# Head 0's q and k joined on SBUF, its turned tile read four times, and eleven heads with values in split halves instead of four

## The chip, the cores and the metric

One core of a Trainium2 chip runs the whole program. The metric is device time in microseconds of one execution; three executions of the kernel before gave a median of 781.59 us (781.08 to 782.19). The core's engines are TensorE (PE in the tables, its weight loads PEld), VectorE (DVE), ScalarE (ACT), GpSimd (POOL) and SyncE (SP, which here only issues DMAs).

## The reference

The program is an attention with a hash mask, followed by two feed-forward blocks on the 1536 tokens that it gives.

```python
q_bits = (einsum('bhsd,dk->bhsk', q, proj) > 0)        # 6 bits each, of q and of k
mask   = q_bucket[:, :, :, None] == k_bucket[:, :, None, :]
scores = where(mask, q @ k.T / sqrt(64), -1e9)         # 2 batches x 8 heads, 768 x 768
attn   = softmax(scores); y = attn @ v                 # head dim 64
x = y as 1536 x 512
h = x @ w_in; g = h * tanh(softplus(h)); x = g @ w_out         # 512 -> 2048 -> 512
out = ((x @ w1) * (x @ w2)) @ w3 @ w_out2                      # 512 -> 1024 -> 1024 -> 512
```

## The kernel before

Heads are counted from 0 to 15. For each head `load_head` brings q and k side by side into one SBUF tile `rw` (128 rows of 6 x 2 x 64), and `prep` makes the features: TensorE turns the tile (L514) so that q stands on the lower 64 partitions and k on the upper 64; a high and a low part are cut from the turned tile (`hh` and `ll`, both in tiles named `hh`, L532 and L534); six DMAs move halves of these into `qb`, `kb`, `qa`, `ka` (L480); three matmuls per half with `psel2` give the hash bits (L565), which VectorE compares (L576) into further rows of `qa`, and one more DMA copies these rows to `ka`. Head 0 has a form of its own (L547 to L555): ScalarE and VectorE write its features straight from the turned tile, in twelve reads, and its bits take four matmuls per half with a matrix `psel`.

`scores` computes one of six row blocks of a head (L606: two matmuls `kb,qb` and two `ka,qa` of 384 columns), VectorE takes the row maximum (L619) and ScalarE the exponential with its row sum (L622). `unit` turns three blocks of `E` (L666) and copies the 128 x 384 result `T` out of PSUM; either ScalarE or VectorE copies (L443). `values` multiplies by v (L695) in one of two forms. A head in the list `FRV` (the bits of `fm`) has split halves: T is copied as a rounded high part, VectorE subtracts the low part (L675), v is cut into high and low columns of one tile (L475), and a pair of T blocks takes four matmuls with 128 stationary columns. Any other head has two matmuls in plain fp32 with 64 stationary columns each, one into the lower and one into the upper 64 rows of the result; the trace shows two records for each of these.

Beside the heads runs work that doesn't depend on them: weights come in as 1 MB chunks and are decoded to fp32 (`decode`, L733 to L747), stored, fetched again and cut into high and low parts (`split`, L796 and L798); `wprod` multiplies w3 and w_out2 (L846); `ff_first` does the feed-forward of the first 512 tokens (L1049, L1065, L1160) while later heads are still at work. The remaining 1024 tokens follow (L1005, L1419, L1461).

The order on every engine is fixed at build time by a planner (`Plan`): each unit of work has a cost, a due time and the buffers that it needs, and the planner places units one by one. Each engine then runs its list strictly in order. The numbers in `CFG` set due times, buffer limits and penalties, so a change of one of them can reorder the lists of all engines.

```python
FRV = [x for x in range(NH) if CFG["fm"] >> x & 1]       # 120: heads 3 to 6
P.op("PE", 0.70 if u in FRV else 0.93, mm, ...)          # values, a pair of T blocks
```

Of the kernel before, what the change touches and what calls it, by code (L numbers as in the profile page):

```python
# [8 lines left out]
F32 = mybir.dt.float32  # L9
# [29 lines left out]
    "hl": 3,  # L39
# [13 lines left out]
    "eg": 0,  # L53
    "xqd": 120.04,
# [5 lines left out]
    "fm": 120,  # L60
# [260 lines left out]
def kernel(  # L321
# [88 lines left out]
    psel = ctile([128, 2, 2, 128], "psel", FR)  # L410
# [11 lines left out]
    v_id, v_psel, v_psel2, v_ccol, v_qks = Val(), Val(), Val(), Val(), Val()  # L422
# [62 lines left out]
    def prep(u, d0, step):  # L485
# [39 lines left out]
        if u:
            for x in ((slice(0, 2), ) if t.one else (slice(0, 1), slice(1, 2))):
                n = (x.stop - x.start) * HS
                cols = slice(x.start * HS, x.stop * HS)
                key = t.all()[x]
                src = (lambda t=t: t.v[0]()[:, :, 0:HS]) if t.one else (lambda t=t, x=x: t.at(x.start))  # L530
                dst = (lambda v_: half(v_())) if t.one else (lambda v_, cols=cols: v_()[:, cols])
                P.op("ACT", act(n) + 0.01, lambda src=src, dst=dst: nc.scalar.activation(  # L532
                    out=dst(hh), in_=src(), func=AF.Copy, scale=qks[:, 0:1]), r=key + [v_qks], w=[(hh, x.start)], due=d(1.3), name=f"hh{u}")
                P.op("DVE", dve(n), lambda src=src, dst=dst: nc.vector.scalar_tensor_tensor(  # L534
                    out=dst(ll), in0=src(), scalar=qks[:, 0:1], in1=dst(hh), op0=ALU.mult, op1=ALU.subtract),
                    r=key + [(hh, x.start), v_qks], w=[(ll, x.start)], due=d(1.6), name=f"ll{u}")
            for o, to, f, fr in ((qb, low, hh, low), (kb, high, hh, high), (qa, low, hh, low), (ka, low, hh, high),
                                 (qb, high, ll, low), (kb, low, ll, high)):
                move(o, to, f, fr, [f], [(o, to.start if o in (qb, kb) else "x")], d(2.2), f"fa{u}")
            ops = [(psel2[:, 0], hh), (psel2[:, 1], hh), (psel2[:, 0], ll)]  # L540
            needs = [hh, ll, v_psel2]
        else:
            inv = 1.0 / float(D) ** 0.5
            for a in range(2):
                cols = slice(a * HS, (a + 1) * HS)
                for o, p, fr, c in ((kb, high, high, inv), (ka, low, high, inv), (qb, low, low, 1.0)):
                    P.op("ACT", act(HS), lambda t=t, o=o, p=p, fr=fr, c=c, a=a, cols=cols: nc.scalar.activation(  # L547
                        out=o()[p, cols], in_=t.at(a)[fr], func=AF.Copy, scale=c), r=[t.key(a)],
                        w=[(o, ("x" if o is ka else p.start, a))], due=d(1.3 + 0.3 * a), name=f"hh{u}")
                P.op("DVE", dve(HS), lambda t=t, a=a, cols=cols: nc.vector.tensor_copy(out=qa()[low, cols], in_=t.at(a)[low]),  # L550
                     r=[t.key(a)], w=[(qa, ("x", a))], due=d(1.3 + 0.3 * a), name=f"hh{u}")
                P.op("DVE", dve(HS), lambda t=t, a=a, cols=cols: nc.vector.tensor_sub(
                    out=qb()[high, cols], in0=t.at(a)[low], in1=qa()[low, cols]), r=[t.key(a), (qa, ("x", a))],
                    w=[(qb, (D, a))], due=d(1.4 + 0.3 * a), name=f"ll{u}")
                P.op("DVE", dve(HS), lambda t=t, a=a, cols=cols: nc.vector.scalar_tensor_tensor(  # L555
                    out=kb()[low, cols], in0=t.at(a)[high], scalar=inv, in1=kb()[high, cols],
                    op0=ALU.mult, op1=ALU.subtract), r=[t.key(a), (kb, (D, a))], w=[(kb, (0, a))], due=d(1.5 + 0.3 * a), name=f"ll{u}")
            ops = [(psel[:, 0, 0], qb), (psel[:, 1, 0], kb), (psel[:, 0, 1], qb), (psel[:, 1, 1], kb)]
            needs = [qb, kb, v_psel]
# [7 lines left out]
        for a in range(2):  # L567
            r = needs if u else [(qb, (x, a)) for x in (0, D)] + [(kb, (x, a)) for x in (0, D)] + [v_psel]
# [18 lines left out]
        for a in range(2):  # L587
# [3 lines left out]
                 r=[(qa, ("m", a))], w=[(ka, ("m", a))], due=d(4.6), name=f"km{u}")  # L591

# [34 lines left out]
    def norm(u, due):  # L627
# [25 lines left out]
        P.op("SP", 0.5, lambda: nc.sync.dma_start(  # L653
# [161 lines left out]
    def wprod(f, d0, d1):  # L815
# [40 lines left out]
        P.op("SP", 0.5, lambda: nc.sync.dma_start(out=wp_d[f * 128:(f + 1) * 128], in_=o()[:, 0:DM]), r=[o], w=[(v_wp, f)],  # L856
# [9 lines left out]
    def x_split(n, due, after=()):  # L866
# [3 lines left out]
        for kk in range(KD):  # L870
# [5 lines left out]
            for e in range(2):  # L876
                P.op("SP", 0.5, lambda e=e, kk=kk, rb=rb: nc.sync.dma_start(
# [62 lines left out]
    def x_quarters(due, after=()):  # L940
        xs = []
        for i in range(2):
            xq_ = Quarters()
            xs.append(xq_)
            for n in (1, 2):
                t0, t1 = n * TB, (n + 1) * TB
                bs = range(t0 // S, (t1 - 1) // S + 1)
                for k1 in range(2):
# [5 lines left out]
                    for e in range(2):  # L954
                        P.op("SP", 0.5, lambda e=e, kk=kk, rb=rb, t0=t0, t1=t1: nc.sync.dma_start(
# [114 lines left out]
    def ff_first(n, d0, d1):  # L1070
# [107 lines left out]
        def o_group(G):  # L1178
# [3 lines left out]
            for t4 in range(TB // 128):  # L1182
# [360 lines left out]
```

## Time and profile before

| | us |
|---|---|
| median of three executions | 781.59 |
| the profiled execution, own time | 781.81 |
| its span | 780.0 |
| PE busy | 765.0 |
| DVE busy | 557.8 |
| ACT busy | 508.9 |

The page gives for each engine the time in which it had an instruction running. TensorE's instructions overlap, so its busy time says only when it was not empty: how fast it went is read from the distance between starts. VectorE's and ScalarE's records overlap by a little as well. The first matmul of head 0's scores starts at 14.8 us, that of head 1 at 28.3, of head 3 at 67.0, of head 7 at 174.4, of head 9 at 213.1, of head 12 at 299.2 and of head 15 at 386.9; the table of stretches in the rows below is cut at these times.

### The profile page before, as it was taken

Reading aid. Unit: us, or ns where it says so; the run is one execution under the profiler, and the core shown is the slowest. Engines: PE = TensorE matmul, PEld = TensorE weight load, DVE = VectorE, ACT = ScalarE, POOL = GpSimd, SP = SyncE. Lnnn points to the kernel's source line nnn. Section 1 sums busy time; section 2 is a strip of 40 time slices with the busy share of each in tenths; the row PEclk is TensorE's granted clock in tenths of the full one; section 3 lists DMA queues with packets and bytes.
Section 4 is the critical chain, followed back from the end, with each engine's and each line's share of the span. In section 5 each row is a group of like instructions: output and inputs, shape, how many; then the busy total and the mean of one; then the engine's idle time right before and its main releaser. Section 6 shows DMA issues by size and latency. Waiting matters only on the chain.

```text
span 780.0 us, 10577 instructions
## 1 busy us (share of the span) xinstructions
PE 765.0 (98%) x3808; PEld 596.7 (76%) x3808; DVE 557.8 (72%) x812; ACT 508.9 (65%) x815; POOL 105.4 (14%) x204
## 2 busy tenths in 40 slices
PE   6999999999999999999999999999999999999998
PEld 5767888897577777777766888888888888788877
DVE  3897778889877986967996959764543848775620
ACT  3889667779799887868867835654544626443330
POOL 3222001222332222113212110000000000000000
PEclk8999999999999999999999999999999999999999
DMA  6997646697897768755465740431215310010011
GB/s 206 214 305 229 181 128 200 157 336 218 259 280 220 249 207 255 230 175 165 158 230 203 259 147 28 162 103 39 75 54 162 109 54 1 28 54 1 1 54 55
DMA packets 62252, 120.70 MB, mean 155 GB/s; under 512 B 29924, under 2 KB 32324, under 8 KB 61176
## 3 DMA queue, kind: packets, MB, share of 16 engines
q1 hardware_dynamic: 45944, 55.02, 25.4%
q0 software_dynamic: 16256, 65.02, 24.2%
q8 instruction: 30, 0.49, 0.3%
q14 instruction: 22, 0.18, 0.1%
HBM read 83.89 MB, written 17.87 MB: 130 GB/s over the span
## 4 chain that ended last, share of the span: by engine, by line
PE 91%; DVE 4%; ACT 2%; issue 1%; DMA 1%; SPq 0%; ACTq 0%; DVEq 0%
PE q L1005 20%; PE b L1419 11%; PE b L1065 9%; PE s L606 8%; PE b L695 8%; PE b L666 7%; PE b L1160 6%; PE b L1049 5%; PE b L846 5%; PE b L1461 5%; PE s L565 2%; PE s L514 1%; PE b L829 1%; DVE st L619 1%; DMA ka<-qa 1%
## 5 line engine op out<-in xcount | busy, mean ns | idle before, releaser
L1005 PE MATMUL q<-k,k 128*128 128x512 f32 x672 | 159.4, 395 | 0.0
L1005 PEld LDWEIGHTS q<-k,k 128*128 128x128 f32 x672 | 126.1, 188 | 30.4 <-DVE f L1020 0.4
L798 DVE TENSOR_TENSOR k<-f,k 128x1024 fp32r<-128x1024 f32 x92 | 111.7, 1220 | 20.5 <-ACT k L796 20.2
L796 ACT CAST k<-f 128x1024 fp32r<-128x1024 f32 x92 | 94.7, 1050 | 21.0 <-DVE f L988 6.4
L619 DVE TENSOR_REDUCE st<-s 128x1 f32<-128x768 f32 x96 | 90.9, 950 | 21.7 <-PE s L606 19.4
L622 ACT ACTIVATE E<-s,st 128x768 f32<-128x768 f32 x96 | 86.9, 905 | 25.1 <-DVE st L619 15.2
L666 PE MATMUL b<-ident,E 128*128 128x128 f32 x576 | 92.0, 274 | 0.2 <-DVE T L675 0.2
L1016 ACT COPY f<-q 128x512 f32<-128x512 f32 x64 | 37.5, 586 | 81.6 <-PE q L1005 78.6
L1020 DVE TENSOR_TENSOR f<-q,f 128x512 f32<-128x512 f32 x64 | 42.9, 686 | 65.8 <-PE q L1005 39.5
L1419 PE MATMUL b<-k,k 128*128 128x512 f32 x384 | 89.6, 393 | 0.0
L666 PEld LDWEIGHTS b<-ident,E 128*128 128x128 f32 x576 | 71.4, 140 | 23.7 <-issue 7.2
L1419 PEld LDWEIGHTS b<-k,k 128*128 128x128 f32 x384 | 72.1, 188 | 16.6
L1065 PE MATMUL b<-k,k 128*128 128x512 f32 x288 | 78.2, 404 | 0.0
L1065 PEld LDWEIGHTS b<-k,k 128*128 128x128 f32 x288 | 51.5, 188 | 15.2 <-issue 6.0
L695 PE MATMUL b<-T,v 128*64 128x384 f32 x288 | 62.4, 511 | 0.0
L606 PE MATMUL s<-kb,qb 128*128 128x384 f32 x192 | 56.7, 376 | 1.4 <-ACT E L622 1.1
L1049 PE MATMUL b<-k,k 128*128 128x512 f32 x192 | 54.5, 407 | 0.0
L443 ACT COPY T<-b 128x384 f32<-128x384 f32 x94 | 43.9, 483 | 15.2 <-PE b L666 13.8
L846 PE MATMUL b<-k,k 128*128 128x512 f32 x192 | 52.1, 405 | 0.0
L606 PE MATMUL s<-ka,qa 76*128 76x384 f32 x192 | 49.9, 341 | 0.6 <-DMA ka<-qa 0.6
L1160 PE MATMUL b<-k,k 128*128 128x512 f32 x192 | 47.4, 396 | 0.0
L1461 PE MATMUL b<-k,f 128*128 128x512 f32 (+1 forms) x216 | 46.4, 370 | 0.8 <-ACT f L1451 0.5
(143 smaller groups left out, 1117.7 us busy)
## 6 DMA issues: line engine op xcount, KB each, us to landing
k<-in_moe_w_dram POOLq DMA_DIRECT2D x16, 1024.0 KB, 5.9
k<-in_moe_w_out_dram POOLq DMA_DIRECT2D x12, 1024.0 KB, 7.8
k<-in_moe_w_in_dram POOLq DMA_DIRECT2D x8, 1024.0 KB, 8.0
f<-keep_wo SPq DMA_DIRECT2D x16, 512.0 KB
qb<-hh SPq DMA_DIRECT2D x30, 192.0 KB
kb<-hh SPq DMA_DIRECT2D x30, 192.0 KB
keep_wi<-f POOLq DMA_DIRECT2D x8, 512.0 KB, 7.0
f<-keep_wi POOLq DMA_DIRECT2D x8, 512.0 KB, 7.0
```

The source lines that it names most:

```text
L606: nc.tensor.matmul(t()[:, a, 0:HS], lhsT=l()[0:kk, i * 128:(i + 1) * 128], rhs=r()[0:kk, a * HS:(a + 1) * HS], start=(l is qb), stop=(l is ...
L619: P.op("DVE", 0.868, lambda: nc.vector.tensor_reduce(out=s()[:, 0, i:i + 1], in_=t()[:, :, 0:HS], axis=AX.XY, op=ALU.max, negate=True), r= ...
L666: nc.tensor.transpose(t()[:, ci * 128:(ci + 1) * 128], es[ci]()[:, kt * 128:(kt + 1) * 128], ident)
L695: nc.tensor.matmul(t()[r, 0:HS], lhsT=w, rhs=f(), start=first and j == 0, stop=last and j == CH - 1)
L796: P.op("ACT", act(1024, True), lambda: nc.scalar.copy(out=hl()[:, 0:1024], in_=f()), r=[f], w=[(hl, 0)], due=due, name="hi")
L798: vec(0, 1024, lambda v_: v_.tensor_sub(out=hl()[:, 1024:2048], in0=f(), in1=hl()[:, 0:1024]), r=[f, (hl, 0)], w=[(hl, 1)], due=due + 0.1, ...
L846: nc.tensor.matmul(acc(), lhsT=hv()[:, ws, g_, :], rhs=wview(wo2[g_ // 2], 2)[:, rs, g_ % 2, :], start=(n == 0), stop=(n == 3 * GT - 1))
L1005: nc.tensor.matmul(qs[q](), lhsT=lhs(w, i), rhs=xs[i].at(xs[i].hl[x], o), start=first and n == 0, stop=n == 5, skip_group_check=True)
L1049: nc.tensor.matmul(of(), lhsT=wview(w, KD)[:, ws, kk, (f % 2) * 128:(f % 2) * 128 + 128], rhs=kview(xhl[n][kk // 2], xs, kk), start=(m == ...
L1065: nc.tensor.matmul(of(), lhsT=l(), rhs=rr(), start=(m == 0), stop=(m == len(ops) - 1))
L1160: nc.tensor.matmul(t(), lhsT=wview(w, KD)[:, ws, kk, f2 * 128:f2 * 128 + 128], rhs=kview(x2[kk // 2], xs, kk), start=(kk == 0 and s == 0), ...
L1419: nc.tensor.matmul(t(), lhsT=wview(w, 2)[:, ws, f, dd * 128:(dd + 1) * 128], rhs=gv[:, gs, f, :], start=(j == 0 and f == 0 and s == 0), st ...
```

## The change

Head 0's q and k are loaded as whole rows into one tile `f`, and two VectorE copies join them into `rw`. Head 0 then goes the way of all other heads: its turned tile is read four times (two halves of `hh` by ScalarE, two of `ll` by VectorE), its bits take three matmuls per half with `psel2`; `psel` is gone, and `psel2` is filled by GpSimd from `proj`. The four halves of `qb` and `kb` are copied by ScalarE and VectorE, those of `qa` and `ka` are moved by DMA. Heads 2 to 6 and 8 to 13 have values in split halves (`fm` 16252), eleven heads. Other numbers of `CFG` change too, so that the planner's order is another on every engine; `low` 29 gives w3's chunks the decoding with two VectorE operations and w_out2's the one with one, where `low` 30 had it the other way.

```diff
-    "prep": 11.28,
-    "wp0": 16.52,
-    "wp1": 41.2,
-    "dec0": 47.78,
-    "dec1": 116.06,
+    "prep": 10.55,
+    "wp0": 16.46,
+    "wp1": 45.62,
+    "dec0": 40.08,
+    "dec1": 121.7,
...
-    "hl": 3,
+    "hl": 4,
...
-    "pen": 0.4,
-    "low": 30,
+    "pen": 0.19,
+    "low": 29,
...
-    "fm": 120,
+    "fm": 16252,
...
+            if u == 0:
+                row = lambda x=x: f()[:, x * C * D:(x + 1) * C * D].rearrange("p (c d) -> p c d", c=C)
+                P.op("SP", 0.65, lambda row=row, src=src: nc.sync.dma_start(
+                    out=row(), in_=src[b, h].rearrange("(p c) d -> p c d", c=C)), w=[(f, nm)], due=due, lat=1.5, name=f"load{nm}{u}")
+                P.op("DVE", dve2(C * D), lambda x=x, row=row: nc.vector.tensor_copy(out=t()[:, :, x], in_=row()), r=[(f, nm)],
+                     w=[(t, nm)], due=due, name=f"join{u}")
+                continue
...
-            for a in range(2):
-                cols = slice(a * HS, (a + 1) * HS)
-                for o, p, fr, c in ((kb, high, high, inv), (ka, low, high, inv), (qb, low, low, 1.0)):
-                    P.op("ACT", act(HS), lambda t=t, o=o, p=p, fr=fr, c=c, a=a, cols=cols: nc.scalar.activation(
-                        out=o()[p, cols], in_=t.at(a)[fr], func=AF.Copy, scale=c), r=[t.key(a)],
-                        w=[(o, ("x" if o is ka else p.start, a))], due=d(1.3 + 0.3 * a), name=f"hh{u}")
...
-            ops = [(psel[:, 0, 0], qb), (psel[:, 1, 0], kb), (psel[:, 0, 1], qb), (psel[:, 1, 1], kb)]
...
+        for o, to, f, fr, e in ((qb, low, hh, low, "ACT"), (kb, high, hh, high, "ACT"), (qa, low, hh, low, ""), (ka, low, hh, high, ""),
+                                (qb, high, ll, low, "DVE"), (kb, low, ll, high, "DVE")):
+            w = [(o, to.start if o in (qb, kb) else "x")]
+            if u or not e:
+                move(o, to, f, fr, [f], w, d(2.2), f"fa{u}", None if u else 2.0)
+            else:
+                P.op(e, act(S, True) if e == "ACT" else dve2(S), lambda o=o, to=to, f=f, fr=fr, e=e: copy(e, o()[to], f()[fr]), r=[f], w=w,
+                     due=d(2.2), name=f"fa{u}")
+        ops = [(psel2[:, 0], hh), (psel2[:, 1], hh), (psel2[:, 0], ll)]
```

What stands on VectorE at the start of the program, before the first row maximum, in the kernel before (`s_74` is the turned tile of head 0, `s_75` its bits):

```order
L1244 COPY ccol<-b_67 128x2
L550 CAST qa_89<-s_74 64x384
L1249 CAST pq<-prow 128x6
L1250 TENSOR_TENSOR pq<-prow,pq 128x6
L1251 TENSOR_SCALAR pq<-pq 128x12
L1255 COPY psel<-pq 128x2x6 x4
L552 TENSOR_TENSOR qb_85<-s_74,qa_89 64x384
L555 SCALAR_TENSOR_TENSOR kb_87<-s_74,kb_87 64x384
L550 CAST qa_89<-s_74 64x384
L555 SCALAR_TENSOR_TENSOR kb_87<-s_74,kb_87 64x384
L552 TENSOR_TENSOR qb_85<-s_74,qa_89 64x384
L576 TENSOR_SCALAR qa_89<-s_75,ccol 64x384 x2
```

And in the changed kernel, in the same place:

```order
L456 COPY rw_95<-f_148 128x6x64 x2
L1238 COPY ccol<-b_67 128x2
L542 SCALAR_TENSOR_TENSOR hh_94<-s_74,qks,hh_93 128x384 x2
L442 COPY qb_85<-hh_94 64x768
L442 COPY kb_87<-hh_94 64x768
L570 TENSOR_SCALAR qa_89<-s_75,ccol 64x384 x2
L614 TENSOR_REDUCE st_106<-s_74 128x1
```

The six reads of the turned tile by VectorE have become two, with the two joins ahead of them and two copies behind them; ScalarE's six reads have become two as well.

TensorE in head 11, around one pair of the values of head 10, before:

```order
L666 MATMUL b_70<-ident,E_84 128x128
L695 MATMUL b_67<-T_2769,v_97 64x384
L695 MATMUL b_67<-T_2796,v_97 64x384
L1065 MATMUL b_68<-k_2468,k_2594 128x512 x3
L1065 MATMUL b_69<-k_2468,k_2594 128x512 x3
```

And in the changed kernel (`f_2791` holds v in two parts):

```order
L601 MATMUL s_75<-ka_92,qa_90 128x384 x2
L690 MATMUL b_70<-T_2839,f_2791 128x384
L690 MATMUL b_70<-T_2849,f_2791 128x384
L690 MATMUL b_70<-T_2855,f_2791 128x384
L690 MATMUL b_70<-T_2872,f_2791 128x384
L661 MATMUL b_69<-ident,E_79 128x128
```

Two matmuls of 64 stationary columns have become four of 128, of the same 384 columns.

VectorE in head 11, from its first row maximum, before:

```order
L619 TENSOR_REDUCE st_108<-s_75 128x1
L443 COPY T_2753<-b_67 128x384
L1125 TENSOR_TENSOR k_2542<-b_70,k_2542 128x512
L443 COPY mvs<-b_68 64x1
L443 COPY T_2769<-b_67 128x384
L619 TENSOR_REDUCE st_108<-s_74 128x1
```

And in the changed kernel:

```order
L614 TENSOR_REDUCE st_108<-s_74 128x1
L670 TENSOR_TENSOR T_2849<-b_67,T_2839 128x384
L442 CAST T_2855<-b_69 128x384
L793 TENSOR_TENSOR k_2821<-f_2414,k_2821 128x1024
L670 TENSOR_TENSOR T_2872<-b_69,T_2855 128x384
L442 CAST T_2876<-b_67 128x384
L633 RECIPROCAL st_107<-st_107 128x6
L670 TENSOR_TENSOR T_2883<-b_67,T_2876 128x384
L1120 TENSOR_TENSOR k_2631<-b_68,k_2631 128x512
L614 TENSOR_REDUCE st_108<-s_75 128x1
```

Between two row maxima there now stand eight operations where four stood.

## Rows read from the trace of the kernel before

**Rows 1.** The page: span, and busy time of the engines.

```profile
span 780.0 us, 10577 instructions
PE 765.0 (98%) x3808; PEld 596.7 (76%) x3808; DVE 557.8 (72%) x812; ACT 508.9 (65%) x815; POOL 105.4 (14%) x204
```

**Rows 2.** Busy by stretch: PE, PEld, DVE, ACT, POOL; clock, DMA share, GB/s.

```profile
0.00:14.80 14.80, 7.38 (x23) 5.56 (x24) 4.25 (x14) 4.50 (x8) 6.76 (x28) 0.90 0.56 146
14.80:28.30 13.50, 13.50 (x75) 12.04 (x75) 9.97 (x14) 8.93 (x20) 0.00 (x0) 0.86 0.87 248
28.30:67.00 38.70, 37.97 (x225) 25.23 (x223) 35.30 (x49) 35.84 (x68) 11.16 (x21) 1.00 0.91 263
67.00:174.40 107.40, 107.40 (x631) 92.42 (x629) 86.23 (x135) 77.94 (x143) 19.05 (x37) 1.00 0.68 205
174.40:213.10 38.70, 36.94 (x221) 27.02 (x219) 36.88 (x57) 32.12 (x65) 10.34 (x20) 1.00 0.78 242
213.10:299.20 86.10, 85.42 (x450) 61.58 (x449) 65.69 (x90) 76.65 (x117) 22.51 (x38) 1.00 0.80 235
299.20:386.90 87.70, 87.70 (x465) 63.27 (x463) 68.74 (x98) 71.05 (x111) 20.49 (x38) 1.00 0.64 201
386.90:780.00 393.10, 388.67 (x1734) 309.58 (x1732) 250.72 (x359) 201.87 (x289) 15.07 (x24) 1.00 0.27 91
```

**Rows 3.** Timeline of the start: start us, us, engine, line, what.

```profile
5.15 1.51 PE L514 MATMUL s<-ident,rw 128*128 128x128 f32 x6 [1.56 <-DMA rw<-in_k_dram]
6.70 0.48 ACT L547 ACTIVATE kb<-s 64x384 fp32r<-64x384 f32 x1 [4.38 <-PE s L514]
...
12.70 0.55 DVE L552 TENSOR_TENSOR qb<-s,qa 64x384 fp32r<-64x384 f32 x1
...
15.06 1.29 DVE L576 TENSOR_SCALAR qa<-s,ccol 64x384 fp32r<-64x384 f32 x2 [1.80 <-PE s L565]
...
16.40 0.58 ACT L532 ACTIVATE hh<-b,qks 128x384 fp32r<-128x384 f32 x1
...
17.01 0.62 DVE L534 SCALAR_TENSOR_TENSOR hh<-b,qks,hh 128x384 fp32r<-128x384 f32 x1 [0.67 <-ACT hh L532]
...
18.02 0.77 PE L606 MATMUL s<-ka,qa 76*128 76x384 f32 x2
...
18.83 1.82 DVE L619 TENSOR_REDUCE st<-s 128x1 f32<-128x768 f32 x2
```

**Rows 4.** Timeline of TensorE around a plain pair of values, head 9.

```profile
236.36 0.49 PE L666 MATMUL b<-ident,E 128*128 128x128 f32 x3
236.78 0.87 PE L695 MATMUL b<-T,v 128*64 128x384 f32 x4
237.58 0.62 PE L606 MATMUL s<-kb,qb 128*128 128x384 f32 x2
```

**Rows 5.** Timeline of TensorE around a split pair, head 3.

```profile
93.61 0.51 PE L606 MATMUL s<-ka,qa 76*128 76x384 f32 x2
93.96 0.86 PE L695 MATMUL b<-T,f 128*128 128x384 f32 x4
94.66 0.49 PE L666 MATMUL b<-ident,E 128*128 128x128 f32 x3
```

**Rows 6.** The chain that ended last: start us, us, what.

```profile
1.48 3.54 DMA rw<-in_k_dram
...
53.01 0.99 PE b L666 x9
...
175.56 0.93 DVE T L675 x2
...
207.36 6.78 DMA ka<-qa
...
429.94 11.12 PE b L1160 x48
```

**Rows 7.** Groups by line: what, xcount | busy us, mean ns | idle before.

```profile
L744 DVE TENSOR_SCALAR k<-f 128x1024 int32<-128x1024 int32 x4 | 2.8, 698 | 0.7 <-ACT f L733 0.7
```

More of the change, by code (lines that the diff above doesn't have):

```diff
@@ L42 @@
     "hlk": 2,
-    "ahead": 12.45,
-    "clk": 120.94,
-    "pen": 0.4,
-    "low": 30,
-    "vdue": 2.94,
+    "ahead": 10.58,
+    "clk": 126.8,
+    "pen": 0.19,
+    "low": 29,
+    "vdue": 2.6,
     "va": 0,
@@ L52 @@
     "tb": 2,
-    "eg": 0,
-    "xqd": 120.04,
+    "eg": 1,
+    "xqd": 110,
     "p0": 2,
@@ L476, in load_v, with move @@
                  r=[t, (g, "hi")], w=[(g, "lo")], due=u * C + CFG["vdue"] + 0.1, name=f"vl{u}")
-    def move(o, to, f, fr, r, w, due, name):
-        P.op("SP", 0.5, lambda: nc.sync.dma_start(out=o()[to].bitcast(F32), in_=f()[fr].bitcast(F32)),
-             r=r, w=w, due=due, lat=5.0, name=name)
+    def move(o, to, f, fr, r, w, due, name, lat=None):
+        P.op("SP", 0.65, lambda: nc.sync.dma_start(out=o()[to].bitcast(F32), in_=f()[fr].bitcast(F32)),
+             r=r, w=w, due=due, lat=lat or 5.0, name=name)
     first_bits = []
@@ L514, in tr @@
                 nc.tensor.transpose(t.at(a)[:, i * 128:(i + 1) * 128], raw()[:, c].rearrange("p s d -> p (s d)"), ident)
-        hh, ll = (Val(HH, "h"), Val(HH, "l")) if u else (None, None)
-        if u and t.one:
+        hh, ll = Val(HH, "h"), Val(HH, "l")
+        halves = not (u and t.one)
+        if not halves:
             P.op("PE", C * 0.118, tr, r=[raw], w=t.all() + [(hh, "t"), (ll, "t")], due=d(1), name=f"tq{u}", after=first_bits)
@@ L521, in prep @@
                 P.op("PE", CH * 0.118, lambda t=t, a=a: tr(t, range(a * CH, (a + 1) * CH)), r=[raw],
-                     w=[t.key(a)] + ([(hh, "t"), (ll, "t")] if u and not a else []), due=d(1), name=f"tq{u}", after=first_bits if u else ())
+                     w=[t.key(a)] + ([] if a else [(hh, "t"), (ll, "t")]), due=d(1), name=f"tq{u}", after=first_bits if u else ())
         low, high = slice(0, D), slice(D, 2 * D)
         half = lambda v_: v_.rearrange("p (a n) -> p a n", a=2)
[L525 to L543, printed above, removed]
-            for a in range(2):
-                cols = slice(a * HS, (a + 1) * HS)
-                for o, p, fr, c in ((kb, high, high, inv), (ka, low, high, inv), (qb, low, low, 1.0)):
-                    P.op("ACT", act(HS), lambda t=t, o=o, p=p, fr=fr, c=c, a=a, cols=cols: nc.scalar.activation(
-                        out=o()[p, cols], in_=t.at(a)[fr], func=AF.Copy, scale=c), r=[t.key(a)],
-                        w=[(o, ("x" if o is ka else p.start, a))], due=d(1.3 + 0.3 * a), name=f"hh{u}")
[L550 to L557, printed above, removed]
-            ops = [(psel[:, 0, 0], qb), (psel[:, 1, 0], kb), (psel[:, 0, 1], qb), (psel[:, 1, 1], kb)]
-            needs = [qb, kb, v_psel]
@@ new lines, in prep @@
+        for x in (slice(0, 1), slice(1, 2)) if halves else (slice(0, 2), ):
+            n = (x.stop - x.start) * HS
+            cols = slice(x.start * HS, x.stop * HS)
+            key = t.all()[x]
+            src = (lambda t=t, x=x: t.at(x.start)) if halves else (lambda t=t: t.v[0]()[:, :, 0:HS])
+            dst = (lambda v_, cols=cols: v_()[:, cols]) if halves else (lambda v_: half(v_()))
+            P.op("ACT", act(n) + 0.15, lambda src=src, dst=dst: nc.scalar.activation(
+                out=dst(hh), in_=src(), func=AF.Copy, scale=qks[:, 0:1]), r=key + [v_qks], w=[(hh, x.start)],
+                due=d(1.3 + 0.1 * x.start), name=f"hh{u}")
+            P.op("DVE", dve(n), lambda src=src, dst=dst: nc.vector.scalar_tensor_tensor(
+                out=dst(ll), in0=src(), scalar=qks[:, 0:1], in1=dst(hh), op0=ALU.mult, op1=ALU.subtract),
+                r=key + [(hh, x.start), v_qks], w=[(ll, x.start)], due=d(1.4 + 0.1 * x.start), name=f"ll{u}")
@@ L567, in prep @@
         for a in range(2):
-            r = needs if u else [(qb, (x, a)) for x in (0, D)] + [(kb, (x, a)) for x in (0, D)] + [v_psel]
+            r = ([(hh, a), (ll, a)] if halves else [hh, ll]) + [v_psel2]
             P.op("PE", pe(HS, len(ops)), lambda a=a: bits(a), r=r, w=[t.key(a)], due=d(4), name=f"bits{u}")
@@ L591, in prep @@
                  r=[(qa, ("m", a))], w=[(ka, ("m", a))], due=d(4.6), name=f"km{u}")
+        first_bits.append(P.units[-1])
     E, st, et, pv = {}, {}, {}, {}
```

47 lines of the change are left out of this document (20 added, 27 removed).

## The prediction

> **What bounds the kernel now.** I read the page's busy times first, then the table of stretches, then the timeline of the start, then TensorE's timeline around the values. TensorE is never empty for long (765.0 of 780.0), VectorE is busy 557.8 [rows 1]. The stretches say more [rows 2]. From 386.9 on TensorE has 388.7 of 393.1 and VectorE 250.7: a pure TensorE tail, 48 matmuls of 512 columns in 11.12 us, 0.232 each [rows 6]. In heads 3 to 6, 9 to 11 and 12 to 14 TensorE is full, VectorE at 80%, 76% and 78%. In heads 1 to 2 and 7 to 8 VectorE is the fullest or nearly so (35.3 and 36.9 of 38.7). Before 14.8 us there is a wait for head 0's features, and TensorE's clock is granted at a mean of 0.90 there and 0.86 in the next stretch, so part of both ran at the lower of its two levels, after TensorE had sat idle between head 0's pieces.
>
> **The start.** Before: k lands at 1.48 + 3.54 = 5.02 [rows 6], the turning starts at 5.15, the reads of the turned tile run from 6.70 to 12.70 + 0.55 = 13.25, the compare starts at 15.06, the second half of the first scores at 18.02, the first maximum at 18.83 [rows 3]. Twelve reads in 6.55 us is 0.55 each, one after another, although two engines share them.
> Now four reads. ScalarE's cost 0.58 and VectorE's 0.62 on this shape [rows 3], together 2.4 us instead of 6.55: 4.1 saved. The bits lose one matmul in four. Against it, two joins stand behind the loads; their form is not in the trace, so 0 to 1.3 us (two of VectorE's 0.62), and the loads themselves may land 0 to 1 us sooner as whole rows; I take both as even. VectorE has two copies of 768 columns ahead of the compare; bounded by nothing and two reads of 0.62, I take 0.9. The new DMAs of `qa` and `ka` can start when the second ScalarE read ends, at 6.70 + 2 x 0.58 = 7.9. A move of that kind with others in flight took 6.78 us, a first load of the program 3.54 [rows 6], so they land between 11.4 and 14.7. The old gap from the compare to the maximum was 18.83 - 15.06 = 3.8 us; the new compare starts near 6.70 + 2.4 + 0.9 + 0.9 (bits) = 10.9, its maximum near 14.7 or earlier. So the first maximum comes at 12 to 15.3 where it came at 18.83: 3.5 to 6.8 gained. I take 5, near the middle, as both ends are the same wait.
> How much of that reaches head 1 depends on head 1's moves, which follow on the same queue and meet the first weight chunks; VectorE also has one v low part and one half of `ll` more in head 0. Bounds 2 and 6.5; I keep **-5.0**.
> The Trainium skill (PSUM — Partial Sum Buffer, PSUM bank collisions raise a hardware error) says that a dependency is added between two engines that touch one bank and quadrant, reads included. That agrees with the strict turns of the twelve reads. By bank alone the two halves could be read side by side, which would end the four reads some 1.2 us sooner; the trace shows turns across both halves, so the sum doesn't use it.
>
> **Values in split halves, TensorE.** A plain pair: three transposes cost 0.33 (nine in 0.99 [rows 6]), and from 236.36 to 237.58 three of them and the pair take 1.22, so the pair takes 0.89 [rows 4]. A split pair takes 94.66 - 93.96 = 0.70 [rows 5]. Seven more heads have six pairs each: 42 x 0.19 = 8.0 us less for TensorE.
> A page speaks against this part: the Trainium skill (TensorEngine Tiling (Array Packing), Theoretical Speedup) gives a stationary side of 64 up to twofold speed, as two tiles work side by side, and the split form gives that up. By that rule alone TensorE would gain nothing here; the rows have the plain pair slower by 0.19, and I go by them.
>
> **Values in split halves, VectorE.** Twelve subtractions more per head, 84. Two in a row take 0.93, 0.465 each [rows 6]: 39 us. In the order VectorE also gets nine copies of T more (4.2) and seven low parts of v, which have the shape of a T subtraction (3.3). `low` moves four operations of 0.70 to VectorE (2.8, [rows 7]) and four of ScalarE's away. That is about +49 us on VectorE with ScalarE somewhat relieved. Whether this costs anything is decided by stretch; I counted the instructions of each head in both orders, cut at the first maximum on VectorE and the first scores on TensorE.
> Heads 1 to 2: VectorE +5 subtractions, +9 copies, -3 decode operations: 6.5 - 2.1 = +4.4, so 39.7 in a stretch of 38.7 that had 3.4 idle. At least +1, at most +4.4; I take **+2**.
> Heads 3 to 6: 24 matmuls of `wprod` (5.6) and 8 transposes (0.9) move out to later heads, the values stay as they are: TensorE 107.4 to 101. VectorE 86.2 + 6 = 92 is still below. **-6.4**.
> Heads 7 to 8: that work arrives here, TensorE +6. VectorE gets 5 subtractions, a copy, two decode merges (1.1 each), a `split`, a compare, two low parts of w3, a v low part and some of the x work, about +10: 46.8 for a stretch of 38.7 that was 95% busy. It must grow, by 5 to 8; I take **+6.5**.
> Heads 9 to 11: VectorE +34 subtractions and a little, 65.7 + 16.8 = 82.5; TensorE 16 split pairs (11.3) for 17 plain ones (15.1) and small things, 86.1 - 4.1 = 82.0. Both engines need the same; with two us of waiting 84: **-2**, bounds -4 and +2.
> Heads 12 to 14: VectorE 68.7 + 18 = 87, TensorE 87.7 - 2.8 = 84.9: 88, **+0.3**, bounds -3 and +5.
> From head 15 on the order has three matmuls more and three transposes fewer: **+0.4**.
> For heads 7 to 14 that is 46.8 + 82.5 + 87 = 216 busy on VectorE against the 212.5 that the stretch took. The base rows count the end of each record in full, some 0.08 that a next one would cover (0.55 for a read that follows at 0.465), so a VectorE without idle time needs 6 or 7 us less, about 209. I end at 45.2 + 84 + 88 = 217, 4% above that.
>
> **Sum.** -5.0 + 2 - 6.4 + 6.5 - 2 + 0.3 + 0.4 = -4.2. The profiled execution took 781.81, so 777.6; the median shown, 781.59, is 0.2 below that execution, which I don't correct for.
>
> **Rivals.**
> VectorE fits in everywhere, as `split` and x work can wait: all of TensorE's 8.0 comes through beside the start's 5.0, 768.8. For it: VectorE's total after is about 607 of 780. Against it: each engine keeps its list, and a subtraction ahead of a row maximum holds up the next scores.
> The start's gain is lost before head 3: heads 1 and 2 have DMA at 0.91, ScalarE at 35.8 and VectorE at 35.3 of 38.7 [rows 2], and head 1's moves are as late as the weights make them. Then 781.8 + 0.8 = 782.6. Against it: the 4 us come off a chain in which two engines took turns, and DMA stands at 0.56 before 14.8 us [rows 2].
> Slower: VectorE bounds heads 7 to 14. It needs 216 of busy time, and where it was fullest before (heads 7 to 8) it was 95.3% busy, as it waits for transposes and for ScalarE's copy ahead of each subtraction. 216 / 0.953 = 227, 14.5 more than 212.5; with -6.4, +2, +0.4 and -5 that is 787. It decides from the point at which VectorE is busy less than 97.5% there (216 / 0.975 = 221.5, which eats 9.0). For it: eight operations between two maxima in head 11. Against it: head 3 to 6's split heads ran at 80% without stopping TensorE.
>
> **Chances.** The forecast 0.47 (773 to 781), all of TensorE's gain 0.17, the start lost 0.20, slower 0.16. About 0.2% (1.6 us) is what a measurement of this kernel can tell from none. Faster: 0.17 + 0.40 + 0.03 = 0.60; within 0.2%: 0.06 + 0.14 = 0.20; slower 0.01 + 0.03 + 0.16 = 0.20. The range 769 to 786 leaves about half of the first rival and half of the last outside.
>
> **What would show it.** The first maximum at 12 to 15.3 us and head 1's first scores near 23; the `T,f` group on TensorE 264 strong at about 0.18 from start to start; VectorE near 605 in all and above 95% in heads 7 to 14; heads 3 to 6 about 101 us, heads 7 to 8 about 45. I am wrong if head 1 starts after 26, or if TensorE waits for VectorE in heads 9 to 14 by more than a few us.

## The result and the profile after

The changed kernel takes 790.68 us (median of 4 runs, 789.06 to 791.35) where the kernel before takes 781.47 beside it: a ratio of 1.0113, 95% interval 1.0100 to 1.0125. It is slower by 9.2 us; the forecast was 4.2 faster, and the range ended at 786.

The page of the profiled execution after (790.65 us), busy time by engine and the clock in 40 slices, against [rows 1]:

```profile
span 788.9 us, 10671 instructions
PE 766.1 (97%) x3809; PEld 622.2 (79%) x3809; DVE 604.2 (77%) x911; ACT 504.5 (64%) x805; POOL 105.5 (13%) x206
...
PEclk9999999999989999989999999999999999999999
```

VectorE has gained 46.4 us of busy time, near the 49 of the forecast. TensorE has lost none, although each split pair is shorter than the plain one it replaces. The clock row has a fall to 8 in two slices in the middle; the one before had none there.

The same stretches, cut at the first scores of heads 0, 1, 3, 7, 9, 12 and 15 (stretch, its length, PE, PEld, DVE, ACT, POOL busy, clock, DMA share, GB/s), answer [rows 2]:

```profile
0.00:9.30 9.30, 6.28 (x20) 4.98 (x20) 3.11 (x8) 4.30 (x6) 5.54 (x27) 1.00 0.70 171
9.30:26.20 16.90, 14.17 (x75) 12.08 (x75) 10.63 (x15) 8.86 (x19) 1.94 (x5) 0.90 0.93 254
26.20:64.50 38.30, 37.02 (x222) 25.85 (x222) 37.58 (x56) 35.04 (x62) 9.85 (x19) 1.00 0.94 273
64.50:168.10 103.60, 102.55 (x604) 89.53 (x602) 91.69 (x147) 70.12 (x136) 17.47 (x37) 1.00 0.61 194
168.10:214.90 46.80, 43.12 (x253) 33.72 (x251) 45.10 (x72) 40.88 (x73) 13.42 (x27) 1.00 0.99 304
214.90:302.20 87.30, 84.58 (x446) 71.42 (x445) 81.17 (x127) 72.00 (x111) 20.64 (x36) 0.96 0.75 218
302.20:394.10 91.90, 88.59 (x471) 74.66 (x470) 88.56 (x144) 71.16 (x115) 23.31 (x36) 0.96 0.59 179
394.10:788.90 394.80, 389.79 (x1733) 310.01 (x1731) 246.39 (x350) 202.19 (x288) 13.29 (x22) 1.00 0.26 88
```

Read it by differences:

| stretch | before | after | change | forecast |
|---|---|---|---|---|
| to head 1's first scores | 28.3 | 26.2 | -2.1 | -5.0 |
| heads 1 to 2 | 38.7 | 38.3 | -0.4 | +2 |
| heads 3 to 6 | 107.4 | 103.6 | -3.8 | -6.4 |
| heads 7 to 8 | 38.7 | 46.8 | +8.1 | +6.5 |
| heads 9 to 11 | 86.1 | 87.3 | +1.2 | -2 |
| heads 12 to 14 | 87.7 | 91.9 | +4.2 | +0.3 |
| the rest | 393.1 | 394.8 | +1.7 | +0.4 |
| sum | | | +8.9 | -4.2 |

In heads 7 to 14 VectorE is busy 45.10 + 81.17 + 88.56 = 214.8 of 226.0 us, 95.0%.

The start after, from its timeline (start us, us, engine, line, what), answers [rows 3]:

```profile
4.10 1.54 PE L521 MATMUL s<-ident,rw 128*128 128x128 f32 x6 [0.29 <-DVE rw L456]
...
9.23 1.29 DVE L570 TENSOR_SCALAR qa<-s,ccol 64x384 fp32r<-64x384 f32 x2
...
13.21 0.59 PE L601 MATMUL s<-ka,qa 76*128 76x384 f32 x2 [1.80 <-DMA ka<-hh]
...
13.84 0.96 DVE L614 TENSOR_REDUCE st<-s 128x1 f32<-128x768 f32 x1 [3.32 <-PE s L601]
...
15.88 0.95 DVE L614 TENSOR_REDUCE st<-s 128x1 f32<-128x768 f32 x1
...
16.25 2.27 PE L559 MATMUL b<-hh,psel 128*128 128x384 f32 x6
...
19.45 0.96 DVE L614 TENSOR_REDUCE st<-s 128x1 f32<-128x768 f32 x1 [0.21 <-PE s L601]
...
24.65 0.58 ACT L539 ACTIVATE hh<-b,qks 128x384 fp32r<-128x384 f32 x1 [0.48 <-DMA ka<-hh]
...
26.17 0.62 PE L601 MATMUL s<-kb,qb 128*128 128x384 f32 x2 [0.26 <-ACT E L617]
```

A piece of the start's chain of waits, and a stretch of the start (columns as above):

```profile
17.00 7.46 DMA ka<-hh
```

```profile
15.20:18.70 3.50, 2.98 (x11) 3.01 (x12) 2.46 (x5) 2.02 (x5) 0.00 (x0) 0.51 1.09 358
```

The first maximum comes at 13.84 instead of 18.83, 5.0 sooner. Head 1's bit matmuls then stand between head 0's second and third maximum: 15.88 to 19.45 is 3.57 us. The granted clock is at its lower level there: the six bit matmuls take 2.27 us, and 1.29 in the profile of the run without subtractions below, where it isn't. Head 1's first scores wait for head 0's last exponentials, and these stand behind a feature copy of head 2 that waited for head 1's move `ka`, which was under way for 7.46 us.

TensorE in head 9, now with split values, answers [rows 4, 5]: from 238.97 to 239.68 the four matmuls of a pair take 0.71.

```profile
238.97 0.86 PE L690 MATMUL b<-T,f 128*128 128x384 f32 x4
239.68 0.86 PE L1044 MATMUL b<-k,k 128*128 128x512 f32 x3
```

Four stretches of heads 9 and 13 (columns as above), then the matmuls that waited ahead of the two falls, from TensorE's timeline, then two pieces of the chain of waits:

```profile
214.90:223.50 8.60, 7.18 (x39) 5.84 (x37) 8.54 (x12) 4.99 (x11) 5.39 (x8) 1.00 1.01 229
223.50:230.30 6.80, 6.42 (x18) 4.87 (x19) 5.47 (x9) 5.53 (x9) 1.14 (x2) 0.50 1.02 377
...
333.90:339.50 5.60, 3.90 (x23) 3.28 (x21) 5.60 (x9) 4.68 (x9) 2.97 (x6) 1.00 1.01 270
339.50:346.30 6.80, 6.29 (x17) 4.86 (x18) 5.89 (x9) 4.05 (x8) 3.64 (x5) 0.50 0.68 245
```

```profile
221.72 0.62 PE L601 MATMUL s<-kb,qb 128*128 128x384 f32 x2 [0.60 <-ACT E L617]
...
223.75 1.70 PE L661 MATMUL b<-ident,E 128*128 128x128 f32 x6 [1.06 <-DVE T L670]
...
338.33 0.61 PE L601 MATMUL s<-kb,qb 128*128 128x384 f32 x2 [1.49 <-ACT E L617]
```

```profile
226.01 3.78 PE b L1044 x8
...
231.80 1.38 PE b L1044 x6
```

In 8.6 us VectorE is busy for 8.54 and TensorE stands idle for 1.4 of them: scores wait 0.60 for an exponential that follows a late maximum, and transposes wait 1.06, part of it in the next stretch, for a subtraction that still reads the PSUM tile that they write. In the 5.6 us ahead of the second fall scores wait 1.49 for an exponential. Then the granted clock is at its lower level, 1.2 GHz, for 6.8 us from 223.5, and again from 339.5. Eight matmuls of 512 columns take 0.473 each at the lower level, six take 0.230 each after it.

### The profile page after: what moved, and what is told of

Read it like the earlier page. It is cut to its first block, busy times and chain, and to the rows that moved or that the text cites. A ratio compares the mean times of both kernels' runs of the same rounds, so it can differ in the third digit from the quotient of the medians.

```text
span 788.9 us, 10671 instructions
## 1 busy us (share of the span) xinstructions
PE 766.1 (97%) x3809; PEld 622.2 (79%) x3809; DVE 604.2 (77%) x911; ACT 504.5 (64%) x805; POOL 105.5 (13%) x206
## 4 chain that ended last, share of the span: by engine, by line
PE 70%; DVE 19%; DMA 3%; issue 3%; ACT 3%; SPq 1%; POOL 0%; ACTq 0%; DVEq 0%; POOLq 0%
PE q L1000 20%; PE b L1405 11%; PE b L1060 6%; PE b L1155 6%; PE b L1447 5%; PE b L841 5%; PE b L1044 5%; PE b L690 4%; DVE st L614 4%; PE b L661 3%; PE s L601 3%; DVE T L670 3%; DVE T L442 2%; DMA k<-in_moe_w_in_dram 2%; DVE k L793 1%
## 5 line engine op out<-in xcount | busy, mean ns | idle before, releaser
L791 ACT CAST k<-f 128x1024 fp32r<-128x1024 f32 x92 | 94.6, 1048 | 23.5 <-PE b L1060 8.9
L1015 DVE TENSOR_TENSOR f<-q,f 128x512 f32<-128x512 f32 x64 | 42.9, 687 | 67.3 <-PE q L1000 41.4
L1405 PE MATMUL b<-k,k 128*128 128x512 f32 x384 | 90.2, 395 | 0.0
L661 PEld LDWEIGHTS b<-ident,E 128*128 128x128 f32 x576 | 70.8, 141 | 24.5 <-issue 4.8
L670 DVE TENSOR_TENSOR T<-b,T 128x384 fp32r<-128x384 f32 x132 | 70.9, 547 | 6.6 <-ACT T L442 5.6
L1060 PE MATMUL b<-k,k 128*128 128x512 f32 x288 | 74.2, 399 | 0.2
L601 PE MATMUL s<-kb,qb 128*128 128x384 f32 x192 | 54.9, 367 | 7.0 <-ACT E L617 3.5
L690 PE MATMUL b<-T,f 128*128 128x384 f32 x264 | 61.4, 354 | 0.3 <-DVE T L670 0.2
L1044 PE MATMUL b<-k,k 128*128 128x512 f32 x192 | 56.6, 427 | 0.9 <-DVE k L1120 0.7
L841 PE MATMUL b<-k,k 128*128 128x512 f32 x192 | 53.7, 406 | 1.3 <-DVE k L832 1.1
L442 ACT CAST T<-b 128x384 fp32r<-128x384 f32 x76 | 35.6, 479 | 22.5 <-PE b L661 20.9
L690 PEld LDWEIGHTS b<-T,f 128*128 128x128 f32 x264 | 46.4, 192 | 3.0 <-DVE T L670 1.4
```

Source lines behind the costliest of these rows:

```text
L601: nc.tensor.matmul(t()[:, a, 0:HS], lhsT=l()[0:kk, i * 128:(i + 1) * 128], rhs=r()[0:kk, a * HS:(a + 1) * HS], start=(l is qb), stop=(l is ...
L661: nc.tensor.transpose(t()[:, ci * 128:(ci + 1) * 128], es[ci]()[:, kt * 128:(kt + 1) * 128], ident)
L670: P.op("DVE", dve(HS), lambda: nc.vector.tensor_sub(out=f[1](), in0=t()[:, 0:HS], in1=f[0]()), r=[t, f[0]], w=[f[1]], due=due, name=f"TL{u ...
L690: nc.tensor.matmul(t()[r, 0:HS], lhsT=w, rhs=f(), start=first and j == 0, stop=last and j == CH - 1)
L791: P.op("ACT", act(1024, True), lambda: nc.scalar.copy(out=hl()[:, 0:1024], in_=f()), r=[f], w=[(hl, 0)], due=due, name="hi")
L841: nc.tensor.matmul(acc(), lhsT=hv()[:, ws, g_, :], rhs=wview(wo2[g_ // 2], 2)[:, rs, g_ % 2, :], start=(n == 0), stop=(n == 3 * GT - 1))
```

## The experiments

Heads "added" are those that the change gives split values: 2 and 8 to 13. Where it says "order held", every instruction that remains stands where the changed kernel has it (or the kernel before, if that is named).

### The set of split heads alone, planned anew

```
changed kernel:     "fm": 16252,  ->  "fm": 120,
kernel before:      "fm": 120,    ->  "fm": 16252,
changed kernel:     all of the planner's numbers as before
```

> The changed kernel with fm 120, so that only heads 3 to 6 have values in split halves; all else as changed, and the planner makes its own order from it. Theory V (VectorE binds heads 7 to 14 because of the 84 added subtractions): 778 to 783, since VectorE loses some 39 us of work and TensorE gets its 8 us back. Rival P (the other due times of CFG crowd decoding and weight loads, whatever the values do): 787 to 791.

> The kernel before with fm 16252 alone: eleven heads in split halves, the old start, the old CFG otherwise. V: 787 to 794, VectorE busy 95% or more in heads 8 to 14. P: 774 to 780, as TensorE saves 8.0 and nothing else is changed.

> The changed kernel with the whole CFG of before: only head 0's load, features and bits are the new ones. Both theories: 776 to 781, the start's gain of 2 to 5 us and no more. If the start's gain doesn't reach later heads, 781 to 783.

Measured: 794.3 us (ratio 1.0159, 1.0143 to 1.0174), 801.34 (1.0247, 1.0232 to 1.0262) and 788.58 (1.0086, 1.0069 to 1.0102). All three forecasts missed. In the third, which has the start's new code and the old numbers of `CFG`, head 1 starts at 25.6 and keeps 2.7 us of gain, but the planner orders the later heads anew: head 9 takes 36.2 us (211.8 to 248.0) where it took 27.3. The costs that the planner counts with are part of the change too, in the code and not in `CFG` (0.65 for the issue of a DMA by SyncE where it was 0.5), and they stay new in the first and third run. A planner that is run again moves everything, and costs here more than the term that was to be isolated. So these runs say nothing of a single part, and the next ones hold the order.

### No subtractions in the added heads, order held

```
-   nc.vector.tensor_sub(out=f[1](), in0=t()[:, 0:HS], in1=f[0]())
+   None if u in ADDED else nc.vector.tensor_sub(...)
-   fs[x][s]
+   fs[x][0 if u in ADDED else s]
```

The values of the added heads lack the low part of T; TensorE does the same matmuls.

> The changed kernel with its planned order, but the subtractions of the seven added heads (2 and 8 to 13) are not issued, and their matmuls read the high part twice, so these heads lack the low part of the weights' product. TensorE's instructions are the same in number and shape. V: 769 to 777, VectorE falls under 85% in heads 9 to 14, and the clock's dips near 223 and 339 us go. P: 785 or more, since the order and all loads stay.

Measured: 780.69 us (778.96 to 782.03; ratio 0.9983, 0.9971 to 0.9994), 10.0 us less than the changed kernel. Heads 7 to 8, 9 to 11 and 12 to 14:

```profile
167.00:212.70 45.70, 42.70 (x252) 33.83 (x251) 43.58 (x67) 40.65 (x73) 13.63 (x26) 1.00 1.00 306
212.70:296.70 84.00, 81.19 (x446) 69.64 (x446) 67.39 (x96) 71.80 (x111) 19.78 (x38) 1.00 0.81 232
296.70:382.80 86.10, 84.31 (x471) 72.67 (x470) 73.87 (x107) 70.43 (x115) 22.07 (x37) 1.00 0.61 190
```

The clock is at its upper level throughout these stretches. The time lies between the two expectations. The subtractions cost 10.0 us, nearly all of it in heads 9 to 14 (179.2 to 170.1). Even so the kernel beats the one before by 1.3 us only, not by the 5 to 13 that were expected: what the new order does to the other stretches stays.

### Plain values in the added heads, order held

```
-   f = Val(TP, "T", dt=FR if u in FRV else F32), ...
+   f = Val(TP, "T", dt=FR if u in FRV and u not in ADDED else F32), ...
+   if u in ADDED: one plain matmul per chunk, no subtraction (of T or of v)
```

> The changed kernel with its planned order held, but the values of the seven added heads in the plain form: no subtraction, T and v in fp32, two matmuls of 64 stationary columns for a pair. It computes the reference. V (VectorE's subtractions cost more than TensorE's shorter pairs give): 781 to 787, that is below the changed kernel's 790.7, VectorE under 90% in heads 9 to 14. If the split halves gain on balance and only the new order costs: 792 to 798.

Measured: 789.7 us (786.98 to 795.89; ratio 1.0101, 1.0075 to 1.0127), between the two expectations; the interval holds the changed kernel's 1.0113. Heads 9 to 11 and 12 to 14:

```profile
215.20:301.40 86.20, 84.83 (x447) 61.10 (x445) 66.20 (x92) 71.53 (x111) 20.22 (x36) 1.00 0.77 222
301.40:391.10 89.70, 88.58 (x471) 63.25 (x469) 73.02 (x105) 70.76 (x115) 22.40 (x37) 1.00 0.59 183
```

TensorE is busy 173.4 us here in heads 9 to 14, and 165.5 in the run without subtractions: the plain form costs it 7.9 us, and the whole kernel 9.0. So the split values give TensorE what was forecast (8.0), and VectorE's subtractions take 10.0: about even. The Trainium skill (TensorEngine Tiling (Array Packing), Theoretical Speedup) gives the plain form, with its stationary side of 64, up to twofold speed; by that rule TensorE would have gained nothing from the split, and these two runs differ by 7.9. The change's 9.2 us are then not in that exchange but in what came with it, the new order above all, which has 46.4 us in heads 7 to 8 even here. The order was planned for the short pairs; what plain pairs lose by that is not shown.

### Added subtractions in the kernel before, its order held

```
+   after each second copy of T in heads 2 and 8 to 13:
+   nc.vector.tensor_sub(out=scr, in0=f[0](), in1=f[0]())
```

84 subtractions into a tile that nobody reads.

> The kernel before with its order held, and behind every copy of T of heads 2 and 8 to 13 one more VectorE subtraction of the same shape into a scratch tile (from SBUF, so no bank of PSUM is held longer): 84 operations that nothing waits for. V: 787 to 796, as VectorE needs some 207 of the 212.5 us of heads 7 to 14. If VectorE has room: 781 to 784.

Measured: 790.52 us (790.22 to 790.96; ratio 1.0105, 1.0088 to 1.0122), as theory V had it. Heads 7 to 8, 9 to 11 and 12 to 14, against [rows 2]:

```profile
176.40:215.60 39.20, 37.21 (x220) 27.06 (x219) 38.87 (x62) 31.23 (x63) 10.15 (x20) 1.00 0.80 242
215.60:304.40 88.80, 86.65 (x451) 61.34 (x450) 81.41 (x125) 77.38 (x119) 24.72 (x39) 1.00 0.80 229
304.40:396.30 91.90, 88.85 (x465) 63.11 (x463) 84.34 (x131) 71.42 (x111) 20.05 (x38) 1.00 0.59 189
```

39 us of VectorE's work cost 9 us, and VectorE is only 92% busy in heads 9 to 14. It need not be full to cost time, nor does the clock have to fall (1.00 in all three). Nothing waits for the added operations themselves; they make later what stands behind them in VectorE's list. TensorE stands idle for 5.2 us of heads 9 to 14, where it was 0.7 before, and most of its waits there are for VectorE: 1.5 for the compare of a head's bits, 1.4 for additions that empty a PSUM tile. None is for an exponential.

### Weights later, and half the weights

```
+   13 memsets on GpSimd ahead of its first weight load         (first run)
+   only half of each w_in and w_out chunk loaded, the rest 0   (second run)
```

The second computes with those half weights. Order held in both.

> The changed kernel with 13 fills of a scratch tile on GpSimd ahead of the first weight load, so that it starts at about 11 us instead of 7.2; order held. If the early weight chunks slow the moves of head 1's features (the loss of the start's gain): head 1's first scores at 23 to 24.5 us instead of 26.2, total 788 to 790. If not: 26 or later, total 790 to 793.

> The changed kernel with only half of each w_in and w_out chunk loaded (the other half is filled with zeros by GpSimd), so it computes with half of these weights; order held. If DMA binds heads 7 and 8 (its share is 0.99 there): these two heads take 44 us or less instead of 46.8 and the total falls by 2 to 5. If VectorE alone binds there (theory V): 46 to 47 and 789 to 791.

Measured: 791.46 us (ratio 1.0121, 1.0106 to 1.0136), head 1 at 27.1; and 790.21 (1.0099, 1.0075 to 1.0122), heads 7 to 8 in 46.3. In the second run the DMA share in heads 7 to 8 falls from 0.99 to 0.88 and their length by 0.5 only, to what it is with whole loads in three other profiles (46.2 to 46.5), so DMA does not bind them. Neither run says whether the early weights lose the start's gain. The two chunks that the program loads first are of w_out2, which the second run loads whole. In the first run the first chunk went out at 14.25 us, not near 11, and so in the middle of head 1's moves. These had been issued sooner (the last at 17.18 instead of 19.75), but one of them then took longer than the 7.46 of the changed kernel, and head 1's first scores waited 3.87 for it:

```profile
16.41 10.41 DMA kb<-hh
```

### The start's order

```
+   order: bits1 behind S0.2, cmp1 behind max0.2          (first run)
+   and besides: hh2 behind exp0.5                        (second run)
```

In the second run half of head 2's low part is taken from an older tile.

> The changed kernel's order is kept but for head 0: the bit matmuls of head 1 go behind head 0's third scores on TensorE, and head 1's compares behind the third maximum on VectorE. Theory F (the start's gain is lost because head 1's preparation, which waits for head 1's own loads, stands between head 0's second and third scores; the pause from the second to the third maximum is 3.57 us where the others are 1.5): head 1's first scores come at 24.2 to 25.0 us instead of 26.2, and the time falls by 1 to 2 us, to 789. Theory G (head 1's loads and moves set the start, whatever stands between): the later bits make head 1 later, 26.2 to 27.5 us, and the time is the same or 1 us more.

> As the run before, and head 2's feature copies on ScalarE go behind head 0's last exponential. Theory F: head 1's first scores at 23.5 to 24.5 us, near the 23.3 that the forecast implied, the time 788 to 789.5. Theory G: 26 us or later. If head 1 comes early and the time stays at 790 to 791, what the start gives is taken by heads 1 to 8, whose VectorE has no room.

Measured: 789.23 us (786.84 to 792.23; ratio 1.0098, 1.0068 to 1.0128) and 789.13 (786.35 to 795.55; 1.0107, 1.0056 to 1.0157). The intervals hold the changed kernel's own ratio, so no gain in time is shown. The traces are clearer. VectorE and ScalarE in the first of the two:

```profile
15.62 0.95 DVE L621 TENSOR_REDUCE st<-s 128x1 f32<-128x768 f32 x1
16.74 0.96 DVE L621 TENSOR_REDUCE st<-s 128x1 f32<-128x768 f32 x1 [0.18 <-ACT f L449]
...
22.96 0.96 DVE L621 TENSOR_REDUCE st<-s 128x1 f32<-128x768 f32 x1 [0.41 <-PE s L608]
```

```profile
24.20 0.58 ACT L546 ACTIVATE hh<-b,qks 128x384 fp32r<-128x384 f32 x1 [1.49 <-DMA ka<-hh]
24.68 0.89 ACT L624 ACTIVATE E<-s,st 128x768 f32<-128x768 f32 x1
```

The third maximum comes at 16.74 instead of 19.45 and the sixth at 22.96 instead of 24.41. But not all of this is the order's doing. In the changed kernel's profile the clock is at its lower level from 15.2 to 18.7, and in this one it isn't. Three other profiles have the changed kernel's own order up to head 1 and no such fall: that of the run without subtractions above, and those of the two runs with half of them below. In these the third maximum comes at 17.65 to 18.06, about a microsecond later than here, but the sixth at 22.61 to 22.97 and head 1 at 25.6 to 26.0, as here (25.7). So moving the bits alone gave head 1 nothing that shows. From the run without the early subtractions:

```profile
22.61 0.96 DVE L615 TENSOR_REDUCE st<-s 128x1 f32<-128x768 f32 x1 [0.41 <-PE s L602]
```

```profile
25.59 0.62 PE L602 MATMUL s<-kb,qb 128*128 128x384 f32 x2 [1.48 <-ACT E L618]
```

After the sixth maximum ScalarE stands for 1.49 us (1.37 to 1.87 in those three): a feature copy of head 2 waits until head 1's moves have let go of a buffer, and head 0's last two exponentials stand behind it. With that copy moved too, head 1 starts at 24.9, 0.7 to 1.1 sooner than in those three, and now its first scores wait for its own move:

```profile
24.91 0.59 PE L615 MATMUL s<-kb,qb 128*128 128x384 f32 x2 [0.47 <-DMA kb<-hh]
```

So it is head 1's moves that hold the start, first through a buffer and then by themselves: neither theory F, whose 23.5 to 24.5 was missed, nor G as it was put, with 26 or later.

The first run's profile also shows the clock's part, since its order from head 1 on is the changed kernel's. Heads 9 to 11 and 12 to 14:

```profile
214.00:300.80 86.80, 83.43 (x445) 70.41 (x445) 81.13 (x127) 71.98 (x111) 20.67 (x37) 0.98 0.74 220
300.80:390.30 89.50, 86.20 (x471) 72.56 (x470) 88.06 (x144) 71.33 (x115) 22.03 (x36) 1.00 0.60 184
```

Without a fall of the clock heads 12 to 14 take 89.5 us, with one 91.9, at nearly the same VectorE work. Others with all of these subtractions fit: 89.4 without a fall in two more profiles (the second run's and the one with half the weights), 90.3 with a fall of 3.4 us (the one with the weights later).

### Half of the subtractions at a time, order held

The edit of the run without subtractions, with ADDED = (11, 12, 13), then (2, 8, 9, 10).

> The changed kernel's order; the 36 subtractions of heads 11, 12 and 13 are not issued (the matmul reads the high part twice, so their values lack the low part). All 84 cost 10.0 us. Theory V (VectorE is the bound along heads 9 to 14, each subtraction costs its share): 36/84 of it, 4.3 us, less: 786.4; the dip of the clock near 343 us goes, the one near 227 us stays. Theory W (a threshold: once TensorE waits at all, the clock falls and the cost comes with the dips): most of one dip, 6.8 us at half the clock, is won back in heads 12 to 14 alone, 784 to 786.

> The changed kernel's order; the 48 subtractions of heads 2, 8, 9 and 10 are not issued (their values lack the low part). Theory V: 48/84 of 10.0, 5.7 us less: 785.0, the dip near 227 us gone, the one near 343 us left. Theory W: heads 9 to 11 fall from 87.3 to 84 us, heads 7 to 8 hardly at all, 786 to 787.

Measured: 784.62 us (ratio 1.0042, 1.0028 to 1.0056) and 785.0 (1.0031, 1.0012 to 1.0051): 6.1 and 5.7 less than the changed kernel. Heads 12 to 14 of the first, heads 9 to 11 and 12 to 14 of the second:

```profile
301.40:387.40 86.00, 84.21 (x470) 72.63 (x469) 73.89 (x108) 70.52 (x115) 22.02 (x37) 1.00 0.62 192
```

```profile
213.40:296.40 83.00, 81.09 (x447) 69.63 (x445) 68.10 (x97) 71.68 (x111) 20.23 (x37) 1.00 0.79 232
296.40:388.40 92.00, 88.60 (x470) 74.73 (x469) 87.90 (x142) 71.16 (x115) 21.62 (x36) 0.96 0.58 178
```

The cost is local: a stretch is short where its subtractions are gone, and long with a fall of the clock where they stay. The second run fits a share of the cost for each subtraction (785.0 expected), the first the cost that comes with the clock's fall (784 to 786). By the ratios to the kernel before it is 5.5 and 6.4, the other way round, so the two readings aren't told apart. 6.1 + 5.7 = 11.8 against 10.0 for both at once is within what the runs of one kernel differ by.

## Why the prediction was wrong

**The sizes held.** The first maximum was put at 12 to 15.3 and came at 13.84 (12.2 to 14.0 in other profiles of this start, so that it is just the 5 us of the forecast is luck). A split pair was put at 0.70 and takes 0.71; the saving on TensorE was put at 8.0 us, and the two runs with the order held give 7.9 of its busy time in heads 9 to 14 and 9.0 of the kernel. VectorE was put at 605 in all and has 604.2; in heads 9 to 14 it was put at 82.5 + 87 = 169.5 and has 169.7. TensorE in heads 7 to 8 was put at 42.9 and has 43.1.

**The step that failed first** is how two loads make a length: "Both engines need the same; with two us of waiting 84", and 88 in heads 12 to 14. Of the 13.1 us between forecast and result some 7 are there. With 82 to 87 us on each of two engines that hand every tile to each other, 87.3 and 91.9 came out: 7.2 us more, and the subtractions are what makes them, as the stretches take 84.0 and 86.1 without. With a fall half as long in heads 9 to 11 and none in heads 12 to 14 it is 86.8 and 89.5, so at least 2.9 of the 7.2 go with the clock, and at most 4.3 are waits alone. An operation on VectorE was given a price only from some 95% on; the run with subtractions added to the kernel before shows 9 us lost at 92%. The rival named this place and this price (227 us for heads 7 to 14, measured 226.0; 787 for the kernel, which had the start at -5.0) and was given 0.16. What spoke against it, that heads 3 to 6 run split values at 80% without stopping TensorE [rows 2], does not carry over: here VectorE is at 93% and 96%.

**The clock** was in the sum nowhere. It fell only near the start before, where TensorE waits anyway; in the runs of the kernel before, mean clocks from 0.995 to 1.000 go with times that don't differ (781.3 to 783.7). In the changed order the time follows it: 786.84 and 787.8 us at 0.998 and 0.995, 790.66 and 792.23 at 0.989, all of the run with the bits later. So some 4 of the 9.2 us hang on the falls. In the changed kernel they follow waits that the subtractions make, and the profile without these has none. But other waits do it too: the run with the start alone has none of the added subtractions and falls for 6.8 us at 228.8, behind one wait of 3.60 us:

```profile
229.81 4.51 PE L1044 MATMUL b<-k,k 128*128 128x512 f32 x9 [3.60 <-ACT k L890]
```

The runs with plain values spread as well, from 786.98 us at 0.999 to 795.89 at 0.993. What share is cause and what is effect (a run that waits more also loses the clock) the runs don't separate. In the profile of 786.84 us TensorE is busy 760.7 and idle 24.3 us, where it was 765.0 and 15.0 before: it saves 4.3 and waits 9.3 more.

**The start:** "-5.0" was right for the first maximum and wrong for head 1, which got 2.1, or 2.3 to 2.7 in the three profiles without the fall at 15.2. "Bounds 2 and 6.5" held, the middle didn't. What the prediction named and then left out of its sum, that head 1 "depends on head 1's moves", is what held it: a move of 7.46 us, a buffer that it keeps from head 2's copy, and head 0's last exponentials behind that copy. Both signs of being wrong came true: head 1 started after 26, and TensorE stands idle for 6.0 us in heads 9 to 14.

**Heads 3 to 8:** -3.8 and +8.1, together +4.3 where +0.1 was forecast. Of heads 3 to 6, TensorE lost 4.85 us of work, not 6.4, and waits for 1.05. In heads 7 to 8 neither the weights (46.3 with half loaded) nor the subtractions (45.7 without) set the length: of the 8.1 us, 6.2 are TensorE's own work (43.1 for 36.9) and 1.9 more waiting (3.7 for 1.8), of which one wait of 1.6 is for VectorE's low part of a head's features. Heads 1 to 2 went better than forecast (-0.4), as VectorE got 2.3 us there, not 4.4.

**What stays open** is why the new order is some 8 us worse than the old one with plain values in both (789.7 against 781.9 beside it). In the profile with plain values, 5.9 us longer than the one of the kernel before, heads 7 to 8 hold 7.7, heads 9 to 14 2.1 and the rest 1.7; heads 3 to 6 give 2.9 back and the start 2.4. Which of the moved pieces could stay was not tried, because each new plan moved everything, and the new decoding of `low` was not tried alone.

## What to carry to other kernels

Where two engines of nearly equal load hand every tile to each other, don't take the larger load plus a microsecond or two, and don't trust a busy share as the threshold either. Dividing VectorE's time by the 95% that its fullest stretch reached before gives 225 us for heads 7 to 14, near the 226.0 measured; for the kernel before with the subtractions added it gives 214.7, and 219.9 came out, where it was 212.5 without them. In both kernels each of the 84 subtractions cost some 0.1 us on average (10.0 and 9 us), though VectorE was not full. Count as a risk of its own that the engine that now waits loses its clock. And test one part of a change with the order held; a planner run again is another kernel.

## What the runs showed of the hardware

TensorE's clock can fall in the middle of a kernel in which TensorE is 97% busy: twice for 6.8 us to the lower level, after it had stood idle for 1.4 of 8.6 us and for 1.7 of 5.6, its longest single wait there 1.49. In another order it fell for as long behind one wait of 3.60. A matmul of 512 columns takes 0.473 us in a fall instead of 0.230. Heads 12 to 14 take 89.4 to 89.5 us without a fall, 90.3 with one of 3.4 us and 91.9 with one of 6.8. The mean clock differs from run to run of one kernel in this order (0.989 to 0.998 with the bits later), and its times spread by 5.4 us; those of the kernel before spread by 1.1 to 2.4 in four sets.

A move of a head's features from one SBUF tile to another took 7.46 us from its issue at the start of the changed kernel, and one took 10.41 where weight chunks were sent in the middle of the moves.
